# Moving a single-row bias load from the POOL queue to the head of the ACT queue, in a gated mix of a state-space layer and a feed-forward layer

## The chip, the cores and the metric

One Trainium2 chip (trn2); the program runs on one of its cores. The metric is device time in microseconds (us) of one execution. The profile's "span" is a little shorter than the device time (211.5 against 212.76 us in the profiled execution before the change). All comparisons of times below are between executions that the record classes as fast (none more than 1.5% above the fastest of its kernel); single executions, whose state is unknown, are used for where things stand in the profile and not for a verdict on time.

The profile names the engines PE (TensorE's matmuls), PEld (TensorE's weight loads), DVE (VectorE), ACT (ScalarE), POOL (GpSimd) and SP (SyncE). A load is first issued by an engine's queue, and it lands, or completes, when its last data has arrived. W1 is the weight matrix of the first layer.

## The reference, cut to what matters

The input x has 2048 rows of 640 numbers in bf16. The result is `g * a + (1 - g) * b`: `g` is a sigmoid gate per row, `a` a diagonal complex state-space layer (640 states), and `b` a feed-forward layer of width 1728 with a tanh-approximated GELU.

```
dt = exp(log_dt);  Lam_bar = exp(dt * (Lambda_re + 1j * Lambda_im))
Bu = x @ B_bar.T;  h[t] = Lam_bar * h[t-1] + Bu[t]          # 2048 steps
a  = 2 * real(h @ C.T) + x * Dskip
b  = gelu(x @ w1 + b1) @ w2 + b2
```

Four small vectors are used as per-partition scalars: `Lambda_re`, `Lambda_im`, `log_dt` (640 each) and `b1` (1728).

## The kernel before

The small vectors are loaded as rows of one 128x128 tile, `rows`: 5 + 5 + 5 + 13 rows of 128 numbers, and a last row, number 28, for the remaining 64 biases. That last row holds the 64 biases twice, because the tail of the first layer is computed for two blocks of x at once, in partitions 0 to 63 and 64 to 127. One TensorE transpose turns all rows into columns. A small list scheduler in the program orders each engine's queue by dependencies and priority (`prio`, lower is earlier).

```python
# rows is cleared first, by POOL; KP = 5, NF = 14, RT = 28, nmain = 1664, F = 1728, FL = 64
op("rz", "pool", 0.2, (), list(ROWS) + ["b1b"], f_rz, prio=-90)
for i, (nm, (r0, src)) in enumerate(ROWS.items()):          # lre, lim, ldt (5 rows each), b1a (13 rows)
    src = src.rearrange("(k p) -> k p", p=128)
    load(nm, "act", "l_" + nm, rows[r0:r0 + src.shape[0], :], src, [nm], prio=-100 + i, dur=0.4)
load("b1b", "pool", "l_b1b", rows[RT:RT + 1, :].rearrange("o (a p) -> o a p", a=2),
     B_b1[nmain:F].rearrange("(o p) -> o p", o=1).unsqueeze(1).broadcast_to([1, 2, FL]), ["b1b"], prio=-50, dur=1.0)
# ... (cut)
def f_cols():                                               # L431: waits for all five loads
    return inc("pe", nc.tensor.transpose(psC, rows[:, :], ident[:, :]))
op("cols", "pe", 0.3, list(ROWS) + ["b1b", "ident"], [("bank", 7)], f_cols, prio=13.5)
def f_cols1():                                              # L436: the columns, for VectorE and ScalarE
    return inc("dve", nc.vector.tensor_copy(out=cols[:, :], in_=psC[:, 0:RT + 1]))
# ... (cut)
```

TensorE starts with seven warm-up matmuls (L400), transposes part of x (L412), and goes on with the first layer (L622). The columns transpose (L431) stands among these matmuls, so TensorE would stop there if the rows were late. The tables that VectorE computes for the state-space layer are made from the columns.

## Time and profile before

| | before |
|---|---|
| device time, median of 3 | 213.44 us (212.94 to 213.54) |
| span of the profiled execution | 211.5 us |
| TensorE busy | 208.1 us, 98% |
| loads of the five row groups complete | 2.84, 3.98, 4.83, 5.17 us (ACT), 4.65 us (POOL) |
| columns transpose: weights loaded, matmul | 6.74, 6.95 us |

The completions are the last of each load's landing events in the trace, in us from the span's start (the prediction cuts the 5.166 us of the 13 bias rows to 5.16).

The page's busy table and the chain of work that ended last, of the kernel before (busy us, share of the span, number of instructions; then the chain's shares by engine):

```profile
PE 208.1 (98%) x1266; PEld 121.2 (57%) x1276; DVE 189.3 (90%) x264; ACT 111.3 (53%) x201; POOL 3.0 (1%) x11
...
PE 98%; issue 0%; DVE 0%
```

TensorE is busy nearly always, and the chain runs through it. Busy alone proves little; the same chain in order of time does more (start, length, what; kernel before, first 20 us):

```profile
0.78 2.93 PE ps L400 x7
3.71 1.03 PE ps L412 x8
4.74 2.38 PE ps L622 x13
7.12 0.06 PE ps L431
7.17 4.32 PE ps L622 x20
```

The pieces follow each other without a gap, so work on another engine matters only if TensorE comes to wait for it. In this view a piece starts where the one before it ends, so L431 stands at 7.12 us here and, by its own start, at 6.95 us in the timeline. Now that timeline, with the parameter loads and the columns (start, length, engine, line, operation; in brackets the engine's idle time before it and what ended it; ACTq and SPq are the queues' own issuing):

```profile
0.97 0.56 ACTq L326 DMA_DIRECT2D rows<-in_A_Lambda_re_dram  x1
...
1.25 0.96 SPq L326 DMA_DIRECT2D W1sb<-in_B_w_dram  x2
...
1.47 0.67 POOL L326 DMA_DIRECT2D rows<-in_B_b_dram  x1
1.56 0.27 ACTq L326 DMA_DIRECT2D rows<-in_A_Lambda_im_dram  x1
...
1.86 0.31 ACTq L326 DMA_DIRECT2D rows<-in_A_log_dt_dram  x1
...
2.20 0.31 ACTq L326 DMA_DIRECT2D rows<-in_B_b_dram  x1
...
2.55 1.28 ACT L441 ACT_TABLE_LOAD   x1 [2.55 <-issue]
...
6.74 0.10 PEld L431 LDWEIGHTS ps<-ident,rows 128*128 128x128 bf16 x1
6.95 0.22 PE L431 MATMUL ps<-ident,rows 128*128 128x128 bf16 x1
```

The moved load is the one on POOL at 1.47 us. It occupies POOL for 0.67 us, at a time when POOL has nothing else to do. The lines for L431 have no bracket: TensorE did not stand idle for the rows.

### The profile page before, as it was taken

The page shows a single profiled execution, that of the slowest core. Times are in us where ns is not written, and L with a number is a line of the kernel's source. Part 1 is how long each engine was busy: PE and PEld are TensorE (multiplying, and loading weights), DVE is VectorE, ACT ScalarE, POOL GpSimd, SP SyncE. Part 2 cuts the span into 40 slices and gives each one's busy share as a digit, 9 for nine tenths or more (in the row PEclk, how much of TensorE's full clock was granted, in tenths as well). Part 3 has the DMA queues.
Part 4 walks back from the last instruction along what each step waited for, and adds up shares of the span by engine and source line. Part 5 has one row for each costly group of instructions (what it writes and reads, how often), then busy time and mean ns, then how long its engine had stood idle before and what let it go on. Part 6 is the DMA issues. An engine that isn't in the chain of part 4 may idle for free.

```text
span 211.5 us, 3140 instructions
## 1 busy us (share of the span) xinstructions
PE 208.1 (98%) x1266; PEld 121.2 (57%) x1276; DVE 189.3 (90%) x264; ACT 111.3 (53%) x201; POOL 3.0 (1%) x11
## 2 busy tenths in 40 slices
PE   8999999999999999999999999999999999999996
PEld 4444444444567776444466777544446777767775
DVE  2599999999999999999999969899999999899444
ACT  2588556678904334556953333456792444723330
POOL 2000000000000010000000001000000000000000
PEclk9999999999999999999999999999999999999999
DMA  5999699999100013100000014100000000010011
GB/s 164 290 246 183 158 225 300 303 213 197 42 0 3 31 38 120 62 0 0 0 3 0 0 48 143 39 23 3 0 0 2 3 31 31 31 34 0 31 34 62
DMA packets 31350, 16.35 MB, mean 77 GB/s; under 512 B 23144, under 2 KB 30440, under 8 KB 31336
## 3 DMA queue, kind: packets, MB, share of 16 engines
q1 hardware_dynamic: 30960, 14.83, 28.5%
q0 software_dynamic: 320, 1.31, 2.0%
q8 instruction: 10, 0.16, 0.3%
q14 instruction: 4, 0.03, 0.1%
q10 hardware_dynamic: 56, 0.01, 0.0%
HBM read 7.63 MB, written 2.62 MB: 48 GB/s over the span
## 4 chain that ended last, share of the span: by engine, by line
PE 98%; issue 0%; DVE 0%
PE ps L772 27%; PE ps L642 22%; PE ps L821 21%; PE ps L685 20%; PE ps L622 4%; PE ps L400 1%; PE ps L786 1%; PE ps L663 1%; PE ps L412 0%; DVE osb L855 0%; PE ps L431 0%
## 5 line engine op out<-in xcount | busy, mean ns | idle before, releaser
L772 PE MATMUL ps<-W2sb,Gl 128*128 128x320 bf16 x416 | 59.2, 299 | 0.0
L772 PEld LDWEIGHTS ps<-W2sb,Gl 128*128 128x128 bf16 x416 | 40.4, 98 | 17.1 <-issue 1.1
L642 PE MATMUL ps<-xT,W1sb 128*128 128x512 bf16 x215 | 47.5, 379 | 0.3
L821 PE MATMUL ps<-CT,H 128*128 128x320 bf16 (+2 forms) x330 | 45.5, 295 | 0.0
L725 DVE TENSOR_TENSOR_SCAN W<-atab,V 128x1280 bf16<-128x1280 f32 x16 | 44.3, 2811 | 0.3
L685 PE MATMUL ps<-xT,BT 128*128 128x512 bf16 x196 | 43.1, 379 | 0.3 <-issue 0.2
L821 PEld LDWEIGHTS ps<-CT,H 128*128 128x128 bf16 x330 | 31.9, 98 | 11.7
L800 ACT ACTIVATE E<-ps,g1col 128x320 bf16<-128x320 f32 x32 | 16.3, 526 | 39.7 <-PE ps L772 25.6
L642 PEld LDWEIGHTS ps<-xT,W1sb 128*128 128x128 bf16 x220 | 21.5, 98 | 26.0
L649 ACT ACTIVATE Gl<-ps,cols 128x512 bf16<-128x512 f32 x44 | 29.6, 688 | 10.0 <-PE ps L642 10.0
L685 PEld LDWEIGHTS ps<-xT,BT 128*128 128x128 bf16 x200 | 19.4, 98 | 23.5 <-ACT Gt L671 0.4
L694 ACT ACTIVATE U<-ps 128x512 bf16<-128x512 f32 x40 | 23.8, 597 | 15.0 <-PE ps L685 14.9
L832 ACT ACTIVATE E<-ps,gcol 128x320 bf16<-128x320 f32 x30 | 15.8, 527 | 22.6 <-PE ps L821 22.6
L759 ACT ACTIVATE ps<-b2b 128x320 f32<-128x320 bf16 x32 | 14.1, 441 | 1.1
L481 DVE TENSOR_TENSOR osb<-xg,E 128x640 bf16<-128x640 bf16 x15 | 7.3, 487 | 7.9 <-ACT E L832 7.6
L842 DVE SCALAR_TENSOR_TENSOR xg<-xn,gcol,dsk 128x640 bf16<-128x640 bf16 x16 | 13.9, 882 | 0.4
L597 DVE SCALAR_TENSOR_TENSOR scr<-xn,gwb 128x640 bf16<-128x640 bf16 x16 | 13.2, 822 | 0.4
L481 DVE TENSOR_TENSOR H<-H,V 128x1280 bf16<-128x1280 bf16 x16 | 12.5, 821 | 0.3
L481 DVE TENSOR_TENSOR V<-V,W 128x1280 bf16<-128x1280 bf16 x16 | 12.5, 821 | 0.3
L481 DVE TENSOR_TENSOR V<-mr,U 128x2560 bf16<-128x2560 bf16 x8 | 11.9, 1488 | 0.2
L481 DVE TENSOR_TENSOR H<-c,W 128x2560 bf16<-128x2560 bf16 x8 | 11.9, 1488 | 0.2
L481 DVE TENSOR_TENSOR W<-mi,U 128x2560 bf16<-128x2560 bf16 x8 | 11.9, 1483 | 0.0
(80 smaller groups left out, 99.9 us busy)
## 6 DMA issues: line engine op xcount, KB each, us to landing
out_dram<-osb SPq DMA_DIRECT2D x15, 160.0 KB, 1.8
W2sb<-in_B_w_dram SPq DMA_DIRECT2D x1, 2080.0 KB, 8.9
W1sb<-in_B_w_dram SPq DMA_DIRECT2D x5, 256.0 KB, 3.9
xn<-in_A_x_dram POOLq DMA_DIRECT2D x2, 640.0 KB, 4.6
xn<-in_A_x_dram SPq DMA_DIRECT2D x1, 640.0 KB, 7.9
W1sb<-in_B_w_dram SPq DMA_DIRECT2D x1, 480.0 KB, 5.8
W1sb<-in_B_w_dram SPq DMA_DIRECT2D x1, 400.0 KB, 6.5
xn<-in_A_x_dram SPq DMA_DIRECT2D x1, 384.0 KB, 6.0
```

The source lines that it names most:

```text
L481: return inc("dve", nc.vector.tensor_tensor(out=o, in0=a, in1=b, op=o_))
L642: t = nc.tensor.matmul(PS[bank][:, :], W1sb[:, k, jf * 128:(jf + 1) * 128], xT[q][:, k, :], start=(k == 0), stop=(k == KD - 1))
L649: return inc("act", nc.scalar.activation(Gl[q % 2][:, jf, :], PS[bank][:, :], ACT.Gelu_apprx_tanh, bias=b1col[:, jf:jf + 1]))
L685: t = nc.tensor.matmul(PS[bank][:, :], BT[:, ci, kd, k * 128:(k + 1) * 128], xT[q][:, kd, :], start=(kd == 0), stop=(kd == KD - 1))
L694: return inc("act", nc.scalar.activation(dst, src, ACT.Copy, scale=1.0 if ci == 0 else -1.0))
L725: t = inc("dve", nc.vector.tensor_tensor_scan(out=g[:, ci, :], data0=a, data1=v[:, ci, :], initial=0.0, op0=ALU.mult, op1=ALU.add))
L759: return inc("act", nc.scalar.activation(PS[bank][:, 0:HALF], b2b[:, cols], ACT.Copy))
L772: t = nc.tensor.matmul(PS[bank][:, 0:HALF], Gl[q % 2][:, jf, t4 * 128:(t4 + 1) * 128], W2sb[:, jf, cols], start=False, stop=False, skip_gr ...
L800: return inc("act", nc.scalar.activation(E1[c % NE][:, cols], PS[bank][:, 0:HALF], ACT.Copy, scale=g1col[:, c:c + 1]))
L821: t = nc.tensor.matmul(PS[bank][:, 0:n], H[b % NHB][:, ci, k, s * 128:(s + 1) * 128], CT[:, ci, k, cols], start=(i == 0), stop=(i == 2 * K ...
L832: return inc("act", nc.scalar.activation(E2[c % NE][:, cols], PS[bank][:, 0:HALF], ACT.Copy, scale=gcol[:, c:c + 1]))
L842: return inc("dve", nc.vector.scalar_tensor_tensor(out=xg[c % 2][:, :], in0=xn[q % 2][:, c % 4, :], scalar=gcol[:, c:c + 1], in1=dsk[:, :] ...
```

## The change

The intent is to take the one early load off POOL and let the ACT queue, which issues the other parameter rows, issue it first.

```diff
-        load("b1b", "pool", "l_b1b", rows[RT:RT + 1, :].rearrange("o (a p) -> o a p", a=2),
-             B_b1[nmain:F].rearrange("(o p) -> o p", o=1).unsqueeze(1).broadcast_to([1, 2, FL]), ["b1b"], prio=-50, dur=1.0)
+        load("b1b", "act", "l_b1b", rows[RT:RT + 1, :].rearrange("o (a p) -> o a p", a=2),
+             B_b1[nmain:F].rearrange("(o p) -> o p", o=1).unsqueeze(1).broadcast_to([1, 2, FL]), ["b1b"], prio=-101, dur=1.2)
```

The compiled order of instructions differs in this one load only: PE, DVE and SP have the same instructions in the same order.

## The prediction

> **What bounds the kernel now.** TensorE. The busy table has PE at 208.1 of a 211.5 us span (98%); the chain of work that ended last is PE for 98%. In time order it is warm-up matmuls from 0.78 us (2.93 us), eight transposes of x from 3.71, then matmuls from 4.74 to 209.5 us with no gap over 0.16 us. In the first stretch 20 matmuls take 4.32 us, 216 ns each, as in later stretches (25 in 5.40 us): no hidden stall there.
>
> **What the change does.** One instruction moves: the two-packet load of the last bias row (b1b, 1x2x64) leaves the POOL queue and becomes first in the ACT queue, inheriting the wait for the memset of the rows tile. PE, DVE and SP are identical, waits included.
>
> - Removed from POOL: an issue of 0.67 us at 1.46 us. POOL's next work is at 77.7 us (75.6 us idle in the list of waits). Worth 0.
> - Added to ACT: one issue. The four row issues took 0.56, 0.27, 0.31 and 0.31 us; the first probably carries a start cost that the new first one takes over, so the queue grows by about 0.3 us. The last row issue (13 bias rows) moves from 2.20 to about 2.5 us, the first table load from 2.55 to about 2.85, ending near 4.1; ACT then still waits until 7.43 us. Worth 0.
> - Moved: the landings. All rows have one reader, the transpose that makes the columns (weights loaded at 6.74 us). In the trace's landing events b1b completes at 4.65 us and the 13 bias rows at 5.16: b1b was not even the last. After: b1b at about 2.9 (the first ACT row landed 1.87 us after its issue), the 13 rows at about 5.5. The transpose keeps 1.2 us of slack, down from 1.6. Neither landing ends a wait.
>
> The Trainium skill, "DMA: Bandwidth & Descriptors", section "Issuing engines are not separate DMA queues", says that loads started by different engines run on the same 16 DMA engines, so that using several saves only sequencer time for the issue. The trace agrees in kind: POOL's and ACT's packets run amid SyncE's, and what changes is 0.67 against about 0.3 us of issue, on queues that nobody waits for.
>
> **On the critical path: nothing, within 0.1 us.** The tight places are SyncE's: the first piece of x lands at 3.63 us, its transposes begin at 3.67; the first W1 piece lands at 4.28, used at 4.5. Two 128-byte packets sent earlier could jostle those by tens of ns, either way. VectorE's table chain starts with the column copy (7.21 us), after the transpose, and does not move.
>
> **Prediction: 213.4 us (before: 213.44), range 212.8 to 214.0.** Faster by over 2%: 1%. Within 2%: 98%. Slower by over 2%: 1%.
>
> **What would show each step right.** Five row issues on ACT, the first about 0.55 us, four near 0.3; no early DMA on POOL; b1b landing first, the 13 rows at about 5.5; the columns transpose still near 6.74 us without PE idle before it, the copy near 7.2; the chain 98% PE; span within 0.5 us of 211.5.
>
> **What would make it wrong.** The 13 rows landing after 6.7 us: then PE, and VectorE's table chain behind it, would slip one for one; that needs 1.6 us of delay from one 0.3 us issue. SyncE's first loads delayed by the earlier row load, so that the transposes start late. Or a first-use cost of POOL's DMA, now paid by the x load at 77.7 us: its readers come 11.8 us later, its landing takes 4.6, so 7 us of slack absorb it.

## The result, and the profile after

| | before | after |
|---|---|---|
| device time, median of 6 | 213.19 us (212.88 to 213.89) | 213.09 us (212.76 to 213.82) |
| ratio | | 0.9996, 95% interval 0.9972 to 1.0021 |
| span of the profiled execution | 211.5 us | 211.6 us |
| first issue on ACT | 0.56 us | 1.19 us |
| 13 bias rows: issue starts, complete | 2.20, 5.17 us | 3.22, 6.57 us |
| moved load complete | 4.65 us | 3.60 us |
| columns transpose, weights loaded | 6.74 us | 6.90 us |

A ratio is the mean time of one kernel's fast runs over that of the other's of the same rounds, so it is not quite the ratio of the medians. No change in time was measured, to within about 0.3%: every run lies in the predicted range but one, by 0.04 us.

The same timeline lines of the kernel after:

```profile
0.98 1.19 ACTq L326 DMA_DIRECT2D rows<-in_B_b_dram  x1
...
1.25 1.15 SPq L326 DMA_DIRECT2D W1sb<-in_B_w_dram  x2
...
2.20 0.31 ACTq L326 DMA_DIRECT2D rows<-in_A_Lambda_re_dram  x1
...
2.54 0.31 ACTq L326 DMA_DIRECT2D rows<-in_A_Lambda_im_dram  x1
...
2.88 0.32 ACTq L326 DMA_DIRECT2D rows<-in_A_log_dt_dram  x1
3.22 0.39 ACTq L326 DMA_DIRECT2D rows<-in_B_b_dram  x1
3.65 1.28 ACT L441 ACT_TABLE_LOAD   x1 [3.65 <-issue]
...
6.90 0.10 PEld L431 LDWEIGHTS ps<-ident,rows 128*128 128x128 bf16 x1
7.12 0.22 PE L431 MATMUL ps<-ident,rows 128*128 128x128 bf16 x1
```

Three things differ from what the prediction had. The new first issue took 1.19 us and not 0.55. The rest of the ACT queue therefore moved by 1.02 us (2.20 to 3.22) and not by 0.3. And SyncE's two W1 issues, which run at the same time, took 1.15 us together in place of 0.96. The list of waits shows where ACT's extra microsecond went (kernel before, then after: who waited for what, total us, times, longest):

```profile
ACT dtb L441 <- DVE cols L436: 3.6, 1, 3.6
ACT L441 <- issue: 2.5, 1, 2.5
```

```profile
ACT L441 <- issue: 3.6, 1, 3.6
ACT dtb L441 <- DVE cols L436: 2.7, 1, 2.7
```

The line with "issue" is the time in which ACT only issued loads, before its first counted instruction. ACT issued for 1.1 us longer and then waited 0.9 us less for the columns: idle time changed its name.

The chain of the kernel after, in order of time:

```profile
0.78 2.93 PE ps L400 x7
3.71 1.12 PE ps L412 x8
4.83 2.45 PE ps L622 x13
7.28 0.06 PE ps L431
7.33 4.32 PE ps L622 x20
```

The columns transpose came 0.16 us later, in the chain as in the timeline, and again with no wait in front of it. Two questions are left: is the 0.16 us a cost of the change, and how close did the change come to a cost?

### The profile page after: what moved, and what is told of

The parts are those of the page before. It is cut to its first block, busy times and chain, and to the rows that moved or that the text cites. A ratio compares the mean times of both kernels' runs of the same rounds, so it can differ in the third digit from the quotient of the medians.

```text
span 211.6 us, 3140 instructions
## 1 busy us (share of the span) xinstructions
PE 208.2 (98%) x1266; PEld 121.3 (57%) x1276; DVE 189.4 (89%) x264; ACT 111.3 (53%) x201; POOL 2.5 (1%) x10
## 3 DMA queue, kind: packets, MB, share of 16 engines
HBM read 7.63 MB, written 2.62 MB: 48 GB/s over the span
## 4 chain that ended last, share of the span: by engine, by line
PE 98%; issue 0%; DVE 0%
PE ps L772 27%; PE ps L642 22%; PE ps L821 21%; PE ps L685 20%; PE ps L622 4%; PE ps L400 1%; PE ps L786 1%; PE ps L663 1%; PE ps L412 1%; DVE osb L855 0%; PE ps L431 0%
## 5 line engine op out<-in xcount | busy, mean ns | idle before, releaser
L685 PE MATMUL ps<-xT,BT 128*128 128x512 bf16 x196 | 43.1, 379 | 0.3 <-issue 0.2
L685 PEld LDWEIGHTS ps<-xT,BT 128*128 128x128 bf16 x200 | 19.5, 98 | 23.4 <-ACT Gt L671 0.4
```

The costliest lines, as they stand in the source:

```text
L685: t = nc.tensor.matmul(PS[bank][:, :], BT[:, ci, kd, k * 128:(k + 1) * 128], xT[q][:, kd, :], start=(kd == 0), stop=(kd == KD - 1))
```

## The experiments

**The theories on the time.** The main theory: the row loads are off TensorE's chain as long as they land before the columns transpose. Small differences at the start come from something that varies between executions of every kernel. The rival: the longer ACT queue costs a little at the start, and the free POOL gives it back elsewhere.

**The theories on the long issue.** A: the 1.19 us belong to this transfer (one row, two runs of 128 bytes from a repeated source). B: they belong to the first place in the ACT queue, beside SyncE's first loads.

Runs e1 to e4 had five rounds beside the kernel before, on the same chip, as had e5 and e6 in a second set.

### e1_same: the changed kernel again

No edit. 

> The changed kernel again, unedited. Main theory (the row loads are off TensorE's chain, and the 0.16 us by which TensorE's stream started later after the change is the moment at which the matmuls became fast, which varies between executions): ratio to before 0.998 to 1.002; the columns transpose somewhere between 6.7 and 7.1 us. Rival (a cost of the longer ACT issues at the start, cancelled by a gain elsewhere): the transpose again at 6.90 or later. On the first ACT issue: if 1.19 us belongs to this transfer in this place, it is again 1.0 to 1.3 us; if it was chance, it is near 0.56.

Measured: 213.21 us median, before 213.5; ratio 0.9993 (0.9972 to 1.0013). The first ACT issue took 1.19 us again, SyncE's second W1 issue 0.60 us, and the 13 rows completed at 6.60 us. So the issue length is a property of the program. The columns transpose came at 7.35 us, later than in both first profiles and outside the 6.7 to 7.1 us that the main theory gave. In this execution TensorE waited 0.3 us for the first W1 piece, which landed only at 4.91 us. The later start needs the runs below.

### e2_last: the same load at the end of the ACT queue

```diff
-             ..., ["b1b"], prio=-101, dur=1.2)
+             ..., ["b1b"], prio=-50, dur=1.2)
```

> The single-row load is last in the ACT queue in place of first. Theory A (the long issue belongs to the transfer, two 128-byte packets): the first issue, now the first parameter row, takes about 0.56 us as before, the 13 bias rows land at about 5.2 us, and the last issue takes about 1.2 us. Theory B (it belongs to the first place, next to SyncE's first loads): the first issue is again over 0.9 us and the last one near 0.3. Time the same as before in both, 0.998 to 1.002; the rival with a cancelled cost would give a gain of 0.1 to 0.2 us here.

Measured: ratio 0.9983 (0.9962 to 1.0005). The trace has the first issue, now five rows of `Lambda_re`, at 0.57 us, and the last, the moved load, at 0.67 us. That is the length it had on POOL. The interval of the ratio is too wide to tell the rival's gain of 0.1 to 0.2 us from none. So both theories on the issue are half right. This transfer takes 0.67 us to issue, about twice the 0.31 us of five or thirteen rows, on either queue; in the first place it takes 0.5 us more. SyncE's two W1 issues were back at 0.96 us.

### e3_two: two plain loads in place of the repeated source

```diff
-        load("b1b", "act", "l_b1b", rows[RT:RT + 1, :].rearrange("o (a p) -> o a p", a=2), <repeated source>, ["b1b"], prio=-101, dur=1.2)
+        for i in range(2):
+            load(f"b1b{i}", "act", f"l_b1b{i}", rows[RT:RT + 1, i * FL:(i + 1) * FL],
+                 B_b1[nmain:F].rearrange("(o p) -> o p", o=1), [f"b1b{i}"], prio=-102 + i, dur=0.6)
```

> The single-row load is split in two plain loads of 64 elements, without the repeated source, first in the ACT queue. Theory A in the form that the repeated source makes the issue long: each of the two takes 0.3 to 0.6 us. Theory A in the form that few packets make it long (one packet each): both take over 1 us, the 13 rows land at about 7.5 us, TensorE waits about 0.7 us and the time grows by 0.7 us (ratio 1.003). Theory B: the first over 0.9, the second near 0.3 us.

Measured: ratio 0.9984 (0.9964 to 1.0003). The two issues took 0.51 and 0.23 us. The timeline of this kernel merges them into 0.77 us:

```profile
0.97 0.77 ACTq L326 DMA_DIRECT2D rows<-in_B_b_dram  x2
...
1.77 0.27 ACTq L326 DMA_DIRECT2D rows<-in_A_Lambda_re_dram  x1
```

Two loads were issued faster (0.77 us) than the one they replace (1.19 us), and the 13 rows completed at 6.25 us. One run from an unrepeated source is the cheap form: it took 0.23 us where the two-run form takes 0.57 to 0.67 behind other issues. Whether the repeated source or the second run within one row makes it expensive is not separated here.

### e4_none: the load taken away

```diff
-        load("b1b", ...)          # and the last 64 biases stay zero: a slightly wrong result on purpose
```

> The single-row load is taken away from every queue (the last 64 biases are then zero: a slightly wrong result on purpose). This is the most that any placement of this load can give. Main theory: 0.998 to 1.002 of before, TensorE's stream as before. Rival (cancelled cost and gain, or a cost of the load in either place): faster by 0.2 us or more, and the columns transpose earlier than 6.7 us.

Measured: ratio 1.0002 (0.9979 to 1.0024). This bounds what any placement of the load can give: nothing was seen, but the interval is about 0.5 us wide on either side, so the rival's 0.2 us is not excluded by the time. The columns transpose came at 7.48 us, later than in either kernel's first profile and not earlier than 6.7 us as the rival had it, with no such load in any queue. What rules out a gain elsewhere is the table of all profiles below: its last column is the same with the load on POOL, on ACT and absent.

### e5_dummy1 and e6_dummy3: how much room is left

```diff
+        for i in range(1):        # e6: range(3)
+            load(f"dum{i}", "act", f"l_dum{i}", rows[RT + 1 + i:RT + 2 + i, :].rearrange("o (a p) -> o a p", a=2),
+                 <the same repeated source>, [f"dum{i}"], prio=-102, dur=0.02)
         load("b1b", "act", ...)   # as in the changed kernel; the columns transpose waits for the copies too
```

The copies go into unused rows; the result stays right. One copy:

> One copy of the single-row load (same shape, repeated source) into an unused row is put ahead of it in the ACT queue, and the columns transpose waits for it too. By the split into a cost of the first place and a cost of the transfer, the first issue takes 1.19 us again and the second, the same transfer, about 0.67; the 13 rows then land near 7.2 us, where TensorE wants them between 6.7 and 7.3: a wait of 0 to 0.5 us, ratio 1.000 to 1.003. If the repeated source alone made 1.19 us, the second takes 1.19 as well and the rows land near 7.8.

Measured: 213.96 us median, before 213.26; ratio 1.0033 (1.0009 to 1.0056). The two issues took 1.20 and 0.58 us, and the 13 rows completed at 7.16 us. Its profile happened to show no wait for the rows: in that execution the first W1 piece landed only at 5.14 us, which held TensorE for about 0.4 us, and the columns transpose came at 7.84. So the 0.3% is measured, but whether late rows or a late W1 piece made it in each execution is open. Its fastest run is 0.73 us above the fastest of before, its slowest 0.31 above the slowest; this would suit a limit that catches only the executions with an early start, but it is argued and not shown.

Three copies:

> Three such copies ahead. Main theory (the row loads have slack only up to the columns transpose, and past it TensorE pays one for one): three times 0.67 us, the 13 rows land near 8.6 us, TensorE waits 1.2 to 1.9 us before the transpose with its next work behind it, and the time grows by that, 1.2 to 1.9 us (ratio 1.006 to 1.009). A theory in which the row loads never matter gives 0.998 to 1.002; if each copy costs 1.19 us the ratio is 1.012 to 1.017.

Measured: 215.01 us median, before 213.26; ratio 1.0084 (1.0059 to 1.0108). The four issues of this kind took 1.20, 0.57, 0.57 and 0.57 us, and the 13 rows completed at 8.99 us. Some plain five-row loads behind the copies took longer to issue as well (0.55, 0.31 and 1.13 us here, 0.44, 0.47 and 0.32 in e5, against about 0.3), so the form and the first place are not all that sets the length of an issue. The list of this kernel's waits has a new line (line numbers are shifted by three, so L434 is the columns transpose):

```profile
PE ps L434 <- DMA rows<-in_B_b_dram: 2.1, 1, 2.1
```

TensorE's matmuls around the transpose lie 2.51 us apart in place of 0.27. The time grew by 0.0084 of 213.3, which is 1.8 us, within what was expected from a wait paid one for one. So row loads can cost time, past a threshold that the landing of the last row sets. The changed kernel lay on the free side of it in all four of its profiles, but by less than was predicted.

### e7 to e11: does the start vary by itself?

The kernel before (e7, e10, e11) and the changed one (e8, e9), unedited, one look each.

> The kernel before, unedited, for a second profile of it. Main theory: its first 8 us vary as those of the others do: the columns transpose starts between 6.9 and 7.8 us, and from the first projection matmul to the end it takes 192.8 us, as in every run so far, so that the difference of the spans is all in the start. Rival (the later starts come from the moved load): the transpose is again within 0.05 us of 6.95.

> The changed kernel once more, for its start alone. Open: in two of four profiles with the repeated-source load first in the ACT queue the first W1 piece landed late (4.91 and 5.14 us against 4.26 to 4.41 in the seven others). If that load causes it, about half of these profiles show a landing after 4.8 us; if it is chance, it is also seen, or seen in none, with the load elsewhere. The rest as before: columns transpose between 6.9 and 8.0 us, 192.8 us from the first projection matmul to the end.

> As the last: first W1 piece landing after 4.8 us in about half of the profiles if the moved load causes it, else near 4.3 us; first ACT issue 1.19 us; 192.8 us from the first projection matmul to the end.

> The kernel before once more: the first W1 piece lands near 4.3 us if only the moved load makes it late, and may land after 4.8 us if it is chance; 192.8 us from the first projection matmul to the end.

> As the last, for a fourth profile of the kernel before: first W1 piece near 4.3 us if only the moved load makes it late; columns transpose anywhere between 6.9 and 8.0 us; 192.8 us from the first projection matmul to the end.

All profiles side by side, from the trace's start times and landing events (us). The last column is the span less the start of the first B-projection matmul (L685).

| profile | moved load on | first W1 piece lands | 13 rows land | columns weights loaded | columns transpose | span | projection to end |
|---|---|---|---|---|---|---|---|
| before | POOL | 4.28 | 5.17 | 6.74 | 6.95 | 211.45 | 192.79 |
| e7 (before) | POOL | 4.31 | 6.04 | 7.75 | 7.96 | 212.47 | 192.80 |
| e10 (before) | POOL | 4.28 | 5.58 | 7.63 | 7.85 | 212.35 | 192.79 |
| e11 (before) | POOL | 4.24 | 5.80 | 7.47 | 7.68 | 212.19 | 192.80 |
| after | ACT, first | 4.28 | 6.57 | 6.90 | 7.12 | 211.63 | 192.80 |
| e1 (after) | ACT, first | 4.91 | 6.60 | 7.13 | 7.35 | 211.86 | 192.81 |
| e8 (after) | ACT, first | 4.30 | 6.59 | 7.02 | 7.24 | 211.76 | 192.81 |
| e9 (after) | ACT, first | 4.39 | 6.33 | 7.30 | 7.52 | 212.02 | 192.80 |
| e2 | ACT, last | 4.41 | 6.02 | 7.26 | 7.47 | 211.99 | 192.80 |
| e3 | ACT, split | 4.27 | 6.25 | 7.54 | 7.75 | 212.30 | 192.83 |
| e4 | none | 4.41 | 6.29 | 7.27 | 7.48 | 212.00 | 192.80 |
| e5 | ACT, second | 5.14 | 7.16 | 7.62 | 7.84 | 212.38 | 192.83 |
| e6 | ACT, fourth | 4.26 | 8.99 | 9.27 | 9.29 | 213.81 | 192.81 |

Neither e8 nor e9 shows the late landing of the first W1 piece (4.30 and 4.39 us) that was to be seen in about half of such profiles if the moved load causes it.

From the first projection matmul to the end every execution takes the same 192.8 us, to 0.04 us. From the columns transpose to that matmul it is 11.71 us in every one. So the differences between spans arise before the columns transpose, and a gain from the free POOL later on, as the rival has it, could be no more than 0.04 us. Two views of windows show it for the first profiles (busy us of each engine and count, then clock, DMA share and GB/s; the second row begins at the projection), before and after:

```profile
0.00:18.66 18.66, 17.83 (x82) 8.19 (x84) 12.06 (x50) 11.54 (x19) 1.49 (x9) 1.00 0.96 230
18.66:211.50 192.84, 190.25 (x1185) 112.98 (x1192) 177.21 (x215) 99.73 (x183) 1.53 (x2) 1.00 0.25 62
```

```profile
0.00:18.82 18.82, 17.99 (x82) 8.27 (x84) 12.11 (x50) 11.54 (x19) 0.82 (x8) 1.00 0.99 232
18.82:211.63 192.81, 190.25 (x1185) 113.06 (x1192) 177.28 (x215) 99.79 (x183) 1.64 (x2) 1.00 0.25 62
```

And the unedited kernel before, in e7, had the columns transpose at 7.96 us, a whole microsecond after its own first profile, later than in any profile of the changed kernel, and above the 6.9 to 7.8 us that was expected. Its chain in order of time:

```profile
3.72 1.17 PE ps L412 x8
4.89 3.23 PE ps L622 x13
8.12 0.06 PE ps L431
```

The same thirteen matmuls took 3.23 us here and 2.38 us in the first profile, with nothing to wait for. In the trace their starts tell why. In the first profile the 256-column matmuls follow each other at 0.109 us and the 512-column ones at 0.216. In e7 the first four come at 0.213, the next two at 0.427, one at 0.276, and only then at 0.217. TensorE ran at half speed until about 4.4 us in the one execution and until about 6.5 us in the other. In the Trainium skill, "TensorE: Matmul & The Clock Gate", section "What's actually happening", this is a clock gate: TensorE starts at half clock and is released after a busy window of 3.4 us that is free-running, so the moment depends on where in the window the work begins. These traces agree in kind. The spacing changes by a factor of two, and the moment wanders by about 2 us, within one window, while the first warm-up matmul starts at 0.78 us every time. This also accounts for the 0.16 us between the two first profiles: the kernel after reached full speed at 4.84 us and not at 4.39, as the clock records of the two traces say and the spacing confirms, and these 0.45 us at half speed cost up to half of that. In the ten profiles in which TensorE waited neither for W1 nor for the rows (all but e1, e5 and e6), the order of the moments of full speed, 4.39 to about 6.5 us by the spacing, is also the order of the columns transposes, whichever queue has the load. No cost of the longer ACT queue shows at the start.

## Why the prediction was right, and which of its terms were off

- **The time and the range.** Right: 213.4 us predicted, 213.09 measured, ratio 0.9996. The reason given for it, that no wait of TensorE ends with a row load, holds in every profile of both kernels for the matmuls and weight loads. It was closer than the prediction knew, and so in part luck (see the slack below). e4 shows no gain even without the load, to within 0.5 us, and e6 that row loads do cost time once they land too late.
- **POOL's part.** Right: 0.67 us of issue taken away from an idle engine. POOL's next load came at 77.9 us instead of 77.7 and took 0.89 us instead of 0.78, behind a wait for VectorE of over 75 us. It changed nothing, as the 192.8 us show.
- **The step that was mis-sized: "the first probably carries a start cost that the new first one takes over, so the queue grows by about 0.3 us".** The queue grew by 1.02 us. The prediction took one issue to cost what another costs. e2 measures this transfer at 0.67 us with no first place, and e1 and the result at 1.19 us with it. Five rows in the first place take 0.56 us, and 0.27 to 0.32 behind. So the first place adds about 0.25 us to one form and 0.5 us to the other; why is open.
- **"The 13 rows at about 5.5" and "1.2 us of slack".** They landed at 6.57, about 1.1 us later than said, of which 0.72 us come from the queue and 0.39 us from a slower landing (3.35 us from issue to completion, against 2.96 in the one profile used; the four profiles of before have 2.96 to 3.83). The slack, from the landing to the loading of the transpose's weights, was 0.33 us. The four profiles of the changed kernel have 0.33 to 0.98 us, the four of before 1.57 to 2.05. Not all of that is free. The packed traces also hold the instructions with which TensorE's queue waits for semaphores, which the views leave out. In all four profiles of the changed kernel the one for the 13 rows begins 0.03 us after their landing, so the queue, which runs ahead of the matmuls, did stand there; in the four of before it was passed 0.4 to 0.7 us after the landing. In e6, where the matmuls stood still as well, the weights were loaded 0.27 us after the landing. Taking some 0.2 us for this, as the changed kernel has one wait instruction fewer, an estimate of the usable slack is 0.1 us in its first profile. The safe margin was mostly used up, and one more such load (e5) brought a measurable 0.3%.
- **"b1b at about 2.9".** It landed at 3.60, 0.7 us later, of which the longer issue is 0.63 us.
- **"The columns transpose still near 6.74 us".** 6.90, which the repeats show to be within the scatter of either kernel. The prediction named SyncE's loads as the source of small differences and missed the larger one here, the moment at which TensorE reaches full speed.
- **A part left open.** With the load first on ACT, SyncE's second W1 issue took 0.60 to 0.62 us in six profiles of six, against 0.42 in the six that lack it or have it elsewhere unsplit (0.51 with it split). The first W1 piece landed late, at 4.91 and 5.14 us, in two of those six and in none of the other seven. That may be chance. If it is an effect, it costs a few tenths of a microsecond in some executions, and the twelve timed runs of the changed kernel, 0.9996 and 0.9993 of before, do not show it.

No version beats both kernels. The split load of e3 is the tidier one on ACT, but its 0.9984 has 1 in its interval.

## What to carry to other kernels

Ask first whether anything waits for the load. A transfer that nobody waits for can move between queues for nothing, but count the slack that the move consumes at the reader, with the issue time of that very transfer in its new place. A 256-byte load took nearly four times as long to issue as its neighbours here. When a difference of a few tenths of a per cent turns up between two profiles, take a second profile of the unchanged kernel before explaining it, and look for the point after which all executions take the same time: only what comes before that point can differ.

## What the Trainium skill lacked or had wrong

- "DMA: Bandwidth & Descriptors", section "Issuing engines are not separate DMA queues", calls the issue time usually small beside the transfer. It says nothing of its dependence on form, place and queue. For these loads of 128 bytes to 3 KB the issue took 0.23 us (one run), 0.27 to 0.32 (five rows, where no copies stood ahead), 0.57 to 0.67 (one row of two runs from a repeated source), 0.51, 0.56 and 1.19 us for the same three forms in the first place of the ACT queue, and up to 1.13 (five rows, behind three copies), against 1.5 to 4.1 us from the start of the issue to the landing.
- The same section names the 16 DMA engines as what the issuing engines share, and no effect of one engine's issue on another's. Here a long issue on ACT went with a longer issue on SyncE at the same time: 0.60 to 0.62 in place of 0.42 us. No page gives a number for this, and why it happens is not shown.
- "DMA: Bandwidth & Descriptors", section "SWDGE vs HWDGE vs iDMA", gives the hardware path of ACT and SP the faster setup. For the moved load the issue was no shorter on ACT: 0.67 us on POOL, 0.67 last on ACT, 1.19 first. From the start of the issue to the landing it took 3.19, 3.69 and 2.62 us.
- "TensorE: Matmul & The Clock Gate", section "What's actually happening", explains the start in kind, but gives the moment of full speed a scatter of ±500 ns. In these thirteen profiles it lay between 4.39 and about 6.5 us. The window view does not show it: it counts time without a clock record as full speed, and has 1.00 for the first 18 us of executions in which the matmuls ran at half speed until about 4.4 us, and likewise where it was about 6.5 us. Only four of the thirteen traces hold a clock record, which begins at full speed (4.39, 4.42, 4.84 and 5.05 us). The spread of this kernel's times (212.7 to 213.9 us in 28 runs of the kernel before) is of the size of that start.
